# Attention with experts on one Trainium2 core: the values' products start one iteration later

## The chip, the core and the metric

The kernel runs on one core of a Trainium2 chip. The metric is device time in microseconds (us) for one execution; lower is better. The engines are named as in the profile: PE is TensorE (matrix products, with PEld for its weight loads), DVE is VectorE, ACT is ScalarE, POOL is GpSimd and SP is SyncE, which issues most of the DMAs here.

## The reference

The program is an attention layer, a mixture of experts that sends each token to one of eight experts, and a dense layer. The change lies in the attention, for 4 batches, 8 heads, 576 tokens and a head width of 64, all in float32:

```
scores = scale * q @ k.T                      # per batch and head
thresh = max(scores, axis=-1) - tau
scores = where(scores >= thresh, scores, -1e9)
scores = scores - max(scores)
attn   = exp(scores)
attn   = attn / (sum(attn) + 1e-9)
out    = attn @ v
```

The experts and the dense layer then work on the 2304 rows of 512 that come out. They use the rows of all batches, so most of them can't begin before attention is nearly done.

## The kernel before, in words

**Pairs, units, iterations.** Two heads make a pair, so there are 16 pairs (`NPAIR`), four per batch. The 576 tokens of the queries of a pair are cut into 9 units (`UPP`): units 0 to 7 are 128 queries of one head, unit 8 is the last 64 queries of both heads. `run` (L440) walks over 144 units, two per iteration, in 73 iterations. Nine iterations are two pairs, one period. `k = it % 9` is the place in the period.

**What an iteration emits, in this order.** The order is written out by hand, and each engine works off its own instructions in that order.
- At the start of a pair: the loads of a later pair's keys and queries (`load`, tile F, L123) and values (`load_v`, tile V, four buffers, L127), and a note that the operands of a later pair are to be split on GpSimd (`split`, L142) and placed by four DMAs (`place`, L162 to L165, tiles qT, kA and kB).
- `qk` (L229): the scores of this iteration's two units, on TensorE (L244), into four PSUM banks that two units use by turns. A unit's scores wait until the mask of the unit two before has read the banks.
- `trans` (L316): the transposes of the two units of the iteration before (L330) and, for k = 0, 2, 5 and 7, those of the tail tokens (`trans_tails`, L338).
- `max` (VectorE, L272) and `exp` (ScalarE, L278) of both units; then ScalarE copies the transposes out of PSUM to the tiles AT (L332, L334) and ATt (L357), each with two buffers; then `mask` on VectorE (L302).
- `values(n)` (L391): it takes up to n items from the queue `avq` and emits them.
- Row items (`row_items`, L398): TensorE turns the finished columns xT back into rows (L414), ScalarE copies them (L419), GpSimd scales them and SP writes them to DRAM.
- One piece of splitting on GpSimd, and some items of the side queue (router set-up and, later, the router's small operations on VectorE): one per iteration, up to eight in the last part.
- At the end of the iteration, the items of a half are put at the end of `avq`: when the transposes that it needs have been emitted, at unit 5 for the first half and unit 8 for the second.

**The items of a half.** A half is 288 of a pair's 576 query columns. It has five items (`av_items`, L359): four product items, `main(0)` to `main(3)`, and one closing item, `tail`. A product item is two matrix products, one per head, which appear as four instructions with 128 x 64 weights (L374); all add up in one PSUM tile `av`. The closing item is a product with the tail tokens (L380, two instructions with 128 x 128 weights), and then ScalarE's copy of `av` to xT (L381). The PSUM pool of `av` has one buffer (`P("ps_av", 1, space=PSUM)`, L1064), so `main(0)` of the next half has to wait for that copy. The closing item of an odd pair's second half also puts five row items into `rowq`.

**How many items per iteration.** The quotas are tables. From iteration `IT_LAST` = 54 on, `AVL` and `ROWL` replace `AV` and `ROW`:

```
AV = (2, 2, 3, 3, 2, 2, 3, 2, 1)
ROW = (0, 1, 0, 1, 1, 0, 1, 0, 1)
AVL = (2, 2, 3, 5, 0, 2, 3, 2, 1, 2, 2, 3, 5, 0, 2, 3, 3, 2, 5)
ROWL = (1, 1, 1, 0, 1, 1, 1, 1, 1, 0, 0, 0, 0, 1, 1, 1, 1, 1, 1)
```

A period has 20 items, and `AV` adds up to 20, so the queue repeats itself. The first items are put into it at the end of iteration 3. In the first five iterations some transposes of the identity, written into a tile `av`, keep TensorE at work (`FILL`).

What is left in the queues after `run` is taken by `tail` (L510) while the expert part begins.

Of the kernel before, what the change touches and what calls it, by code (L numbers as in the profile page):

```python
# [24 lines left out]
UPP = 9  # L25
PJ = 9
NPC = 2
AV = (2, 2, 3, 3, 2, 2, 3, 2, 1)
TURNS = ((0, 1), (2, 3))
TAILS = {2: -1, 5: -2, 7: -2, 0: -1}  # L30
IT_LAST = (NPAIR - HP) * UPP // 2
AVL = (2, 2, 3, 5, 0, 2, 3, 2, 1, 2, 2, 3, 5, 0, 2, 3, 3, 2, 5)
# [17 lines left out]
class Attention:  # L50
# [389 lines left out]
    def run(self):  # L440
        nc = self.nc
        NU = NPAIR * UPP
        self.load_first()
        self.load(1)
        rest = self.first()
        self.load_v(0)
        self.load_v(1)
        self.load(2)
        self.poolq = []
        self.avq, self.rowq, self.side = avq, rowq, side = [], [], []  # L450
        side += [None] * NS0 + [self.gate_setup, *self.router.setup_items(self.setup), *self.extra]
        it = done = 0
        while done < NU:
            last = it >= IT_LAST
            us = [u for u in (2 * it, 2 * it + 1) if u < NU]
            ts = [u for u in (2 * it - 2, 2 * it - 1) if 0 <= u < NU]
            starts = [u // UPP for u in us if u % UPP == 0]
            for p in starts:
                if p + 3 < NPAIR:
                    self.load(p + 3)  # L460
                if p + 2 < NPAIR:
                    self.load_v(p + 2)
                for n in range(1 if p == 0 else p + 2, min(p + 3, NPAIR)):
                    self.operands(n)
                    self.poolq += [lambda n=n, i=i: self.split(n, i, NPC) for i in range(NPC)]
            k = it % 9
            for u in us:
                self.qk(u)
            copies = [self.trans(u) for u in ts]
            if it > 1 and k in TAILS:  # L470
                copies.append(self.trans_tails(2 * it + TAILS[k]))
            for i in range(2):
                if i < len(us):
                    self.max(us[i])
                    self.exp(us[i])
                if last:
                    self.sides(SD[i], False)
            for c in copies:
                c()
            while rest:  # L480
                rest.pop(0)()
            if self.norm:
                self.norm.pop(0)()
            for i, u in enumerate(us):
                self.mask(u)
                if last:
                    self.sides(SD[i + 2], False)
            if it < len(FILL) and FILL[it]:
                warm = self.ps_av.tile([128, 512], F32, name="av")
                for _ in range(FILL[it]):  # L490
                    nc.tensor.transpose(warm[:, 0:128], self.ident, self.ident)
            n = AVL[it - IT_LAST] if last else AV[k]
            self.values(n)
            m = ROWL[it - IT_LAST] if last else ROW[k]
            while m and rowq:
                rowq.pop(0)()
                m -= 1
            n = 1 if it else 2
            while n and self.poolq:
                self.poolq.pop(0)()  # L500
                n -= 1
            self.sides(SD[4] if last else SN)
            for u in ts:
                done = u + 1
                p, w = divmod(u, UPP)
                if w in (5, 8):
                    avq += self.av_items(p, w // 8)
            it += 1
# [1074 lines left out]
```

## Time and profile before

| what | value |
|---|---|
| time, median of 3 runs | 964.17 us (961.75 to 965.95) |
| the profiled execution's own time | 964.58 us |
| its span, first to last instruction | 962.8 us |
| mean granted TensorE clock | 0.987 of full speed |
| TensorE busy | 910.0 us, 95% of the span |
| VectorE busy | 510.8 us, 53% |
| ScalarE busy | 446.9 us, 46% |
| GpSimd busy | 223.3 us, 23% |

The profile is that of one execution. Its time is 1.8 us longer than its span, since launch and end lie around the instructions. A share of busy time is an average over the whole span, and attention (to about 348 us) and the expert and dense part behind it have different limits. Matrix products are pipelined and their ends are modelled, so a busy TensorE need not be at its peak. An idle time is put down to what ended it by the semaphores that the instruction waited for; "issue" means that the profile shows nothing that it waited for.

### The profile page before, as it was taken

The numbers are of one execution on the slowest core, as the hardware profiler recorded it, in microseconds if no ns is written. First come the engines' busy times: TensorE is split into PE (matmuls) and PEld (weight loads), VectorE is DVE, ScalarE is ACT, GpSimd is POOL, SyncE is SP. The second block draws the span as 40 slices with busy tenths as digits, with TensorE's granted clock in tenths as the row PEclk, the third lists the DMA queues.
The fourth block names the chain that finished last, engine by engine and source line by source line (L and its number), as shares of the span: only waits on it lengthen the run. The fifth ranks groups of instructions, "written<-read, shape, count | busy, mean of one in ns | idle before, by whom it ended". The sixth has DMA issues, their size and how long they took to land.

```text
span 962.8 us, 13873 instructions
## 1 busy us (share of the span) xinstructions
PE 910.0 (95%) x5031; PEld 744.9 (77%) x5031; DVE 510.8 (53%) x1129; ACT 446.9 (46%) x788; POOL 223.3 (23%) x299
## 2 busy tenths in 40 slices
PE   8899899998898989999999999999999999999995
PEld 7677677776676668877888988888888888888894
DVE  6677677776778748457868658851111111111110
ACT  6566666666666543345555544542222222222221
POOL 4737544566441340101151000001001000100100
PEclk9999999999999989999999999999999999999998
DMA  7655565544440262546574625421001000100100
GB/s 213 161 138 138 161 160 143 149 111 121 118 116 12 67 222 91 183 137 229 181 228 154 240 67 175 127 70 44 22 23 45 1 16 6 44 1 1 44 1 24
DMA packets 64522, 100.70 MB, mean 105 GB/s; under 512 B 10596, under 2 KB 35970, under 8 KB 64450
## 3 DMA queue, kind: packets, MB, share of 16 engines
q1 hardware_dynamic: 61138, 89.84, 32.0%
q0 software_dynamic: 3312, 9.94, 3.2%
q8 instruction: 41, 0.67, 0.3%
q14 instruction: 31, 0.25, 0.1%
HBM read 63.97 MB, written 17.11 MB: 84 GB/s over the span
## 4 chain that ended last, share of the span: by engine, by line
PE 73%; issue 8%; DVE 6%; ACT 6%; DMA 3%; POOL 1%; SPq 1%; POOLq 0%; ACTq 0%
PE tr L993 27%; PE sc L1018 18%; PE sc L1037 8%; PE sc L244 7%; PE av L374 6%; PE tr L330 3%; ACT e L278 3%; DVE e L272 2%; PE tr L414 2%; ACT AT L332 1%; DVE E L302 1%; DVE ET L302 1%; PE av L380 1%; DMA xg<-x_dram,igaA 1%; DVE bl L1263 1%
## 5 line engine op out<-in xcount | busy, mean ns | idle before, releaser
L1230 DVE TENSOR_TENSOR hl<-sg,hh 128x512 fp32r<-128x512 f32 (+1 forms) x80 | 51.0, 638 | 259.8 <-ACT hh L1228 259.8
L278 ACT ACTIVATE e<-e,thr 128x576 f32<-128x576 f32 x144 | 109.9, 776 | 93.3 <-DVE e L272 90.0
L272 DVE TENSOR_SCALAR_CACHE_REDUCE e<-sc,taue 128x576 f32<-128x576 f32 x144 | 113.9, 816 | 66.6 <-PE sc L244 65.4
L1227 ACT ACTIVATE sg<-tr 128x512 f32<-128x512 f32 (+1 forms) x80 | 44.3, 554 | 224.9 <-PE tr L993 224.9
L1018 PE MATMUL sc<-wo_h,hh 128*128 128x512 f32 x288 | 112.2, 390 | 0.0
L1018 PE MATMUL sc<-wo_l,hh 128*128 128x512 f32 x288 | 112.2, 390 | 0.0
L1018 PE MATMUL sc<-wo_h,hl 128*128 128x512 f32 x288 | 112.0, 389 | 0.0
L244 PE MATMUL sc<-kA,qT 128*128 128x288 f32 x320 | 99.5, 331 | 7.2 <-DVE E L302 3.8
L302 DVE SCALAR_TENSOR_TENSOR E<-sc,thr,e 128x576 f32<-128x576 f32 x128 | 101.1, 813 | 5.1 <-ACT e L278 3.8
L374 PE MATMUL av<-AT,V 128*64 128x288 f32 x512 | 76.5, 422 | 22.1 <-ACT xT L381 22.0
L244 PE MATMUL sc<-kB,qT 128*128 128x288 f32 x320 | 89.3, 299 | 2.1 <-DMA kB<-kB 1.2
L244 PEld LDWEIGHTS sc<-kA,qT 128*128 128x128 f32 x320 | 61.0, 191 | 27.9 <-DVE E L302 14.8
L993 PE MATMUL tr<-xl,wi_h 128*128 128x512 f32 (+1 forms) x320 | 78.7, 368 | 0.0
L993 PE MATMUL tr<-xh,wi_l 128*128 128x512 f32 (+1 forms) x320 | 78.7, 368 | 0.0
L993 PE MATMUL tr<-xh,wi_h 128*128 128x512 f32 (+1 forms) x320 | 78.6, 368 | 0.0
L374 PEld LDWEIGHTS av<-AT,V 128*64 128x64 f32 x512 | 31.4, 137 | 49.6 <-ACT xT L381 27.9
L330 PE MATMUL tr<-ident,E 128*128 128x128 f32 x512 | 69.4, 277 | 0.0
L332 ACT COPY AT<-tr 128x512 f32<-128x512 f32 x128 | 68.2, 577 | 0.1
L993 PEld LDWEIGHTS tr<-xh,wi_h 128*128 128x128 f32 x320 | 57.6, 188 | 11.1
L993 PEld LDWEIGHTS tr<-xl,wi_h 128*128 128x128 f32 x320 | 56.9, 189 | 10.0
L993 PEld LDWEIGHTS tr<-xh,wi_l 128*128 128x128 f32 x320 | 56.9, 189 | 10.0
L244 PEld LDWEIGHTS sc<-kB,qT 128*128 128x128 f32 x320 | 61.4, 192 | 2.9 <-DVE kB L223 1.3
(220 smaller groups left out, 1592.4 us busy)
## 6 DMA issues: line engine op xcount, KB each, us to landing
ra<-in_moe_w_dram SPq DMA_DIRECT2D x20, 512.0 KB, 3.6
rb<-in_moe_w_dram SPq DMA_DIRECT2D x20, 512.0 KB, 3.8
F<-in_kq_dram SPq DMA_DIRECT2D x15, 640.0 KB, 4.8
cv_raw<-in_moe_w_in_dram SPq DMA_DIRECT2D x16, 512.0 KB, 4.5
cv_raw<-in_moe_w_out_dram SPq DMA_DIRECT2D x16, 512.0 KB, 4.2
V<-in_vp_dram SPq DMA_DIRECT2D x16, 320.0 KB, 5.0
kA<-kA SPq DMA_DIRECT2D x15, 320.0 KB, 3.3
kB<-kB SPq DMA_DIRECT2D x15, 320.0 KB, 3.6
```

The lines of the kernel that those rows point to most:

```text
L244: m = nc.tensor.matmul(self.banks[:, bank, 0:288], l, d[kk][:, c0 + k0:c0 + k0 + 288], start=(i == 0), stop=(i == len(ops) - 1),).ins
L272: self.read(u, nc.vector.tensor_scalar(e, d["sc", w], self.taue[:, 0:1], 3.0e38, op0=ALU.add, op1=ALU.min, accum_out=thr))
L278: self.nc.scalar.activation(d["e", w], d["e", w], ACTF.Exp, bias=d["thr", w][:, 0:1], scale=-1.0)
L302: self.read(u, nc.vector.scalar_tensor_tensor(out=E.rearrange("p (a c) -> p a c", a=2), in0=d["sc", w], scalar=d["thr", w][:, 0:1], in1=d[ ...
L330: nc.tensor.transpose(tp[:, kc * 128:(kc + 1) * 128], E[:, k0 + kc * 128:k0 + (kc + 1) * 128], self.ident)
L332: return lambda: nc.scalar.copy(AT[:, h, :, c * 128:(c + 1) * 128], tp.rearrange("p (k c) -> p k c", k=4))
L374: nc.tensor.matmul(d["av"][h * 64:(h + 1) * 64, 0:288], d["V"][:, h, kc, :], d["AT"][:, h, kc, cols], start=(kc == 0), stop=False, skip_gr ...
L993: nc.tensor.matmul(hps[:, 0:T], w[:, kd, :], blk[x][:, kd, 0:T], start=(i == 0), stop=(i == 11))
L1018: nc.tensor.matmul(y, h[:, cs], w, start=(f == 0 and i == 0), stop=(f == blk["nf"] - 1 and i == 2))
L1037: nc.tensor.matmul(blk["y"][d], w[:, ds], h[:, 0:T], start=(f == 0 and i == 0), stop=(f == last and i == 2))
L1227: nc.scalar.activation(sg, hps, ACTF.Gelu_apprx_sigmoid)
L1230: return [upper, lambda: nc.vector.tensor_sub(hl, sg, hh.bitcast(F32))]
```

## The change

The call of `values` gets a condition. With `UPP` = 9, `UPP // 2` is 4, so iterations 0 to 4 take nothing from the queue. Before iteration 4 the queue is empty in any case; at iteration 4 the kernel before took two items.

```
--- before.py
+++ after.py
@@ -489,8 +489,8 @@
                 warm = self.ps_av.tile([128, 512], F32, name="av")
                 for _ in range(FILL[it]):
                     nc.tensor.transpose(warm[:, 0:128], self.ident, self.ident)
-            n = AVL[it - IT_LAST] if last else AV[k]
-            self.values(n)
+            if it > UPP // 2:
+                self.values(AVL[it - IT_LAST] if last else AV[k])
             m = ROWL[it - IT_LAST] if last else ROW[k]
             while m and rowq:
                 rowq.pop(0)()
```

The tables are the same, and so is every instruction; what moves is the place of the values' items, and with the closing items that of the row items, in the order of the iterations.

## Rows read from the trace of the kernel before

**Rows 1.** The page's first part: busy time, share and instructions of each engine.
```profile
PE 910.0 (95%) x5031; PEld 744.9 (77%) x5031; DVE 510.8 (53%) x1129; ACT 446.9 (46%) x788; POOL 223.3 (23%) x299
```

**Rows 2.** Waits of TensorE, 28 to 261 us: total us, times, longest.
```profile
PE av L374 <- ACT xT L381: 21.5, 12, 1.9
```

**Rows 3.** Stretches: start:end, length, busy us of engines, granted clock, DMA.
```profile
28.28:261.00 232.72, 208.96 (x1472) 161.76 (x1473) 172.88 (x471) 153.33 (x285) 126.87 (x170) 0.99 0.54 139
348.00:963.00 615.00, 601.16 (x2868) 502.81 (x2867) 259.04 (x437) 225.49 (x380) 53.94 (x65) 0.99 0.27 89
```

**Rows 4.** Timeline, one iteration of k = 2: start, duration, instruction, idle time before.
```profile
97.06 0.65 PE L380 MATMUL av<-ATt,V 128*128 128x288 f32 x2
...
97.78 1.05 ACT L332 COPY AT<-tr 128x512 f32<-128x512 f32 x2
...
98.98 0.42 ACT L381 COPY xT<-av 128x288 f32<-128x288 f32 x1
...
99.46 1.19 PE L374 MATMUL av<-AT,V 128*64 128x288 f32 x8 [1.75 <-ACT xT L381]
```

**Rows 5.** Stretches: iterations k = 0, 2, 6, 7 of one period, and its sum.
```profile
127.76:131.86 4.10, 3.92 (x30) 2.88 (x28) 3.78 (x10) 3.76 (x9) 2.34 (x3) 1.00 0.19 60
...
135.60:141.56 5.96, 4.20 (x29) 2.96 (x28) 3.94 (x11) 3.82 (x9) 4.86 (x5) 1.00 0.34 116
...
153.73:159.93 6.20, 4.48 (x33) 3.27 (x31) 4.06 (x12) 3.82 (x8) 5.81 (x5) 1.00 0.02 3
159.93:163.38 3.45, 3.45 (x29) 2.64 (x28) 2.46 (x7) 2.10 (x4) 1.41 (x3) 1.00 0.80 171
...
sum 39.36, PE 35.69 PEld 27.82 DVE 30.01 ACT 26.41 POOL 20.77; mean PE 3.97 PEld 3.09 DVE 3.33 ACT 2.93 POOL 2.31
```

**Rows 6.** Stretches: iterations 60 (k = 6), 65 (k = 2) and 69 (k = 6).
```profile
274.34:278.55 4.21, 4.21 (x33) 3.30 (x32) 3.13 (x8) 3.03 (x7) 4.03 (x5) 1.00 0.08 19
...
294.98:299.38 4.40, 4.12 (x29) 3.02 (x29) 4.37 (x16) 2.86 (x6) 1.01 (x6) 1.00 0.01 4
...
313.90:318.12 4.22, 4.22 (x33) 3.31 (x32) 4.07 (x17) 2.98 (x6) 0.81 (x2) 1.00 0.14 35
```

**Rows 7.** Timeline of iteration 60 and the start of iteration 61.
```profile
276.45 1.19 PE L374 MATMUL av<-AT,V 128*64 128x288 f32 x8
...
277.56 0.30 PEld L380 LDWEIGHTS av<-ATt,V 128*128 128x128 f32 x2 [0.44 <-issue]
277.57 0.75 PE L380 MATMUL av<-ATt,V 128*128 128x288 f32 x2
...
278.16 0.65 PE L414 MATMUL tr<-G,xT 128*128 128x144 f32 x4
278.44 0.41 ACT L381 COPY xT<-av 128x288 f32<-128x288 f32 x1
...
280.29 0.78 ACT L278 ACTIVATE e<-e,thr 128x576 f32<-128x576 f32 x1 [0.99 <-DVE e L272]
...
280.88 1.19 PE L374 MATMUL av<-AT,V 128*64 128x288 f32 x8
```

**Rows 8.** Line L374 from 266 to 330 us: what its idle time ended with.
```profile
  issue: 1.8, 11
```

**Rows 9.** Stretch: iterations 58 to 66 together.
```profile
265.85:304.09 38.24, 35.76 (x259) 28.00 (x257) 30.58 (x85) 26.89 (x50) 13.40 (x22) 1.00 0.31 72
```

**Rows 10.** Stretches by granted clock, and iteration 7 (k = 7).
```profile
39.20:42.60 3.40, 3.40 (x17) 3.29 (x16) 2.47 (x7) 1.64 (x3) 0.82 (x1) 0.50 0.67 147
...
117.70:121.10 3.40, 3.40 (x16) 2.30 (x13) 0.00 (x0) 0.40 (x1) 1.81 (x3) 0.50 0.50 110
...
261.00:264.40 3.40, 3.40 (x18) 3.06 (x18) 2.49 (x7) 1.55 (x3) 1.51 (x1) 0.51 0.59 127
...
38.79:43.86 5.07, 5.07 (x28) 4.19 (x26) 3.24 (x8) 2.78 (x5) 1.23 (x1) 0.66 0.62 134
```

**Rows 11.** Timeline of SP: the last DMA that places pair 6's operands.
```profile
103.68 0.59 SPq L165 DMA_DIRECT2D kB<-kB  x1
```

More of the change, by code (lines that the diff above doesn't have):

```diff
@@ L491, in run @@
                     nc.tensor.transpose(warm[:, 0:128], self.ident, self.ident)
-            n = AVL[it - IT_LAST] if last else AV[k]
-            self.values(n)
+            if it > UPP // 2:
+                self.values(AVL[it - IT_LAST] if last else AV[k])
             m = ROWL[it - IT_LAST] if last else ROW[k]
```

## The prediction, made before the change was run

> **What bounds the kernel now.** I read the page first: TensorE is busy for 910.0 us of a span of 962.8 [rows 1]. A share of 95% looks as if nothing were left, so I asked next who TensorE waited for in the steady part of attention, 28 to 261 us, where the change lies. One wait heads that list: 21.5 us, 12 times, the first product of a half waiting for ScalarE's copy of the half before (L374 behind L381) [rows 2]. The same stretch as a window has 232.72 us with 208.96 us of TensorE in it [rows 3], so this wait is 21.5 of 23.8 us idle.
>
> The timeline of one such iteration shows how it comes about [rows 4]. The closing product starts at 97.06 and takes 0.65 us, so it is over at 97.7. Its copy to xT stands in ScalarE's queue behind the copies of this iteration's transposes, which start at 97.78, and begins only at 98.98. There is one av bank, so the next half's first product, which follows in the same run, starts at 99.46, after 1.75 us idle. A closing product at the *front* of a run meets ScalarE when it still has the iteration's copies to do.
>
> Last I cut one period of nine iterations (39.36 us) into its iterations [rows 5]. I call them by k, the iteration's number modulo 9. Two are long: k = 2 with 5.96 us and k = 6 with 6.20; the other seven have 27.2 us together, 3.9 each. The long ones are those whose run is "closing, first, second".
>
> **The change part by part.** The queue of the values' items starts one iteration later and stays two items behind. With m for a product item and T for a closing one, the runs of a period were k=0 mm, 1 mm, 2 Tmm, 3 mmT, 4 mm, 5 mm, 6 Tmm, 7 mm, 8 T. They become mT, mm, mmT, mmm, mT, mm, mmT, mm, m. The 20 items are all there, T is always last, and no m follows a T in its own run. At iteration 57 the quota of five takes three items before and five after; from its end on the order is the same in both kernels. So from iteration 58 the trace of before holds iterations in just the new order: my price list.
>
> *k = 6, six iterations.* 6.20 us now [rows 5]. The same items with T last took 4.21 and 4.22 us [rows 6]. Saved 1.98 each, 6 x 1.98 = 11.9.
>
> *k = 2, six iterations.* 5.96 us now, with 4.20 us of TensorE [rows 5]; without the wait 4.20 would be left. The iteration of this k in the new order took 4.40, with 0.28 of TensorE idle [rows 6], while VectorE had small operations of the router to do as well. I take 4.30, between the two: 6 x 1.66 = 10.0 (9.4 to 10.6).
>
> *k = 0, 3, 4 and 8* exchange an m for a T or back. Two m take 1.12 us, from 276.45 to 277.57, so one takes 0.56; a T takes 0.59, from 277.57 to 278.16 [rows 7]. Each exchange is 0.03 us, plus in two and minus in two: nothing. If k = 0 lost its 0.18 us of idle TensorE too [rows 5], that would be 6 x 0.18 = 1.1 more.
>
> As a check: a period becomes 39.36 - 1.98 - 1.66 = 35.7 us. The nine iterations from 265.85 to 304.09, with 20 items in the new order, hold 35.76 us of TensorE in 38.24 [rows 9]. The 2.5 us between are idle, in iterations that run up to eight of the router's items; the steady ones run one.
>
> *The clock.* Three stretches of 3.4 us ran at a granted 0.50 or 0.51, the 1.2 GHz level, and each began during or right behind one of the twelve waits, at 39.20, 117.70 and 261.00 [rows 10]. The first made an iteration of k = 7 last 5.07 us [rows 10] where the same k takes 3.45 at full clock [rows 5]: 1.6 each, 4.8 for three. With no idle of 1.8 us left in front of them I take all three as gone; the other end is 0.
>
> *The two ends.* Iteration 4 loses two m, 1.12 us of TensorE, but its next scores also wait for VectorE's masks; the gain is 0 to 1.1, I take 0.6. Iteration 57 gets two m more, +1.1. One row item moves out of iteration 12 and one into 55: nothing. Together +0.5.
>
> *What I cost at nothing, and what covers it.* (a) The copy to xT now ends each run, ahead of the next iteration's exponentials in ScalarE's queue. In the new order it starts at 278.44 and takes 0.41 us, and the next exponential starts at 280.29, after ScalarE was idle for 0.99 [rows 7]. With that cover gone it would be 0.41 per half, 24 halves, 10 us. (b) The first product of the next run meets a copy long done: at 280.88 no copy is named before it [rows 7], and over the whole late stretch the products waited for "issue" alone, 1.8 us [rows 8]. (c) SP: a pair's V load goes into the buffer of the pair four before the pair loaded, whose last closing product now comes in the load's own iteration, not the one before. SP waits there an iteration longer, about 4 us; behind it stand operand placements, row writes and later loads. The placement issued at 103.68 [rows 11] is for the pair that starts at 127.76 [rows 5], so 24 us early. (d) The AT and ATt buffers (two each) are refilled in the iteration after a pair's last T, behind it on TensorE, which works in order. (e) The row items, and the router's behind them, come an iteration or two later until iteration 57, then at the old places. (f) The expert part, 615 us from 348 on [rows 3], starts from what attention delivers and moves up with it; I find nothing in it tied to absolute time.
>
> One price the notes would add. In the trace a T behind an m has its weight load idle for 0.44 us, but its matmul starts at 277.57, just when eight at 0.14 are through, so TensorE loses nothing [rows 7]. The Trainium skill (TensorE: Matmul & The Clock Gate, Part 3, The mechanism) says that a weight load overlaps matmuls in flight only when the row groups differ, which speaks against full-array products behind half-array ones. One more such switch comes per period (at k = 8): by the rule 6 x 0.44 = 2.6 us and a time near 941; by the row, 0.
>
> **Sum.** -11.9 - 10.0 - 4.8 + 0.5 = -26.2 against this execution's own 964.58 us (its span is 962.8): 938.4. The execution lies 0.4 above the median of the runs shown, 964.17, so 938.
>
> **The rivals.**
> 1. *The clock falls all the same*, there or elsewhere: 964.6 - 21.9 + 0.5 = 943. For: nine of the twelve waits had no fall behind them, so such a wait alone does not decide it. Against: all three falls touch a wait.
> 2. *VectorE takes over.* Periods then look like the 38.24 us of [rows 9], 1.1 saved each: 964.6 - 6.7 - 4.8 + 0.5 = 954. For: VectorE is busy 30.0 us of 39.36 [rows 5] and would be so of 35.7. Against: the steady part has one side item per iteration, and its plain iteration reaches 3.45 [rows 5].
> 3. *The wait only moves* to the next iteration's first product, so that the change does not do what it says: 960 to 965. For: there is still one av bank. Against: the late stretch [rows 8]. The Trainium skill (Perfetto Trace Analysis, Optimizing Tensor Performance, Matmuls) asks that independent groups rotate through banks, so that one's evacuation overlaps the next one's matmuls; by that rule an unrotated bank keeps its wait. The late stretch does not agree: scores and transposes fill the time.
> 4. *Slower: SP's queue.* The V load that waits an iteration longer holds back the operand placements behind it. Place: SP at a pair's start. Price, if a pair's scores had to wait for that iteration: 13 pairs x 4 us = 52, so 938 + 52 = 990. It decides only once the hold exceeds the 24 us by which a placement is early.
>
> **How the numbers follow.** Forecast 0.66, rival 1 0.16, rival 2 0.09, rival 3 0.06, rival 4 0.03. Predicted: 938. The range goes down by 1.1 for k = 0, 0.6 for the end of k = 2 and about 2 for half-clock stretches elsewhere that also touch an idle TensorE: 934. Upward it takes in rival 1 (943) and 4 us of rival 2's waits: 947. About 0.2 is outside. No change means within 0.5%, 4.8 us, about what a measurement can tell: rival 3. Faster 0.91, same 0.06, slower 0.03.
>
> **What would show it.** In the profile after: TensorE's wait for the xT copy gone from the steady part (if it stands before the next iteration's products, rival 3); k = 2 and k = 6 at 4.2 to 4.4 us (longer, and idle behind VectorE's masks: rival 2); no stretch at 0.50 between the first values and iteration 57 (else rival 1); no wait of the scores for an operand's DMA after iteration 4 (else rival 4). The expert part must keep its length; if it changes by more than 2 us, point (f) is wrong.

## The result, and the profile after

The changed kernel takes 936.49 us (934.96 to 938.53, median of 4 runs) against 963.83 us in runs beside it; the ratio is 0.9725 with a 95% interval of 0.9697 to 0.9753. The prediction was 938. The profiled execution took 936.12 us with a span of 934.4, so 28.5 us less than the one of before.

The page's first part of the changed kernel, which answers to [rows 1]: the same instructions, TensorE 6 us less busy.

```profile
PE 904.0 (97%) x5031; PEld 740.6 (79%) x5031; DVE 512.2 (55%) x1129; ACT 446.8 (48%) x788; POOL 223.1 (24%) x299
```

TensorE's waits in the changed kernel from 28.79 to 238.64 us (iterations 5 to 57). This is the whole list; the row of [rows 2] is no longer in it.

```profile
PE sc L244 <- DVE E L302: 0.7, 3, 0.3
PE sc L244 <- DVE ET L302: 0.5, 2, 0.3
PE sc L244 <- issue: 0.2, 1, 0.2
```

The same as stretches (length, then busy us of each engine). The steady part has 1.0 us without TensorE where [rows 3] had 23.8. The second row is the expert and dense part, from its first product to the end.

```profile
28.79:233.92 205.13, 204.10 (x1463) 159.00 (x1463) 173.70 (x469) 152.02 (x283) 123.42 (x165) 1.00 0.62 157
319.45:934.40 614.95, 600.95 (x2867) 502.91 (x2867) 257.63 (x435) 224.94 (x378) 52.33 (x65) 0.99 0.28 89
```

The timeline of the changed kernel's iteration 20 (k = 2), the one of [rows 4].

```profile
89.12 1.19 PE L374 MATMUL av<-AT,V 128*64 128x288 f32 x8
...
89.95 1.06 ACT L332 COPY AT<-tr 128x512 f32<-128x512 f32 x2
...
90.24 0.75 PE L380 MATMUL av<-ATt,V 128*128 128x288 f32 x2
...
90.61 0.51 PE L244 MATMUL sc<-kA,qT 128*128 128x288 f32 x1
...
90.89 0.38 ACT L357 COPY ATt<-tr 128x256 f32<-128x256 f32 x1
...
90.96 0.29 PE L244 MATMUL sc<-kB,qT 128*128 128x288 f32 x1
...
91.16 0.42 ACT L381 COPY xT<-av 128x288 f32<-128x288 f32 x1
```

The closing product (L380) comes after the two product items, and the next scores follow it at 90.61. ScalarE's copy to xT still stands behind its other copies; it starts 0.92 us after the closing product (1.92 in [rows 4]), and TensorE has scores and transposes to do meanwhile.

One period of the changed kernel (iterations 27 to 35, k = 0 to 8), to be read beside [rows 5].

```profile
114.56:118.32 3.76, 3.76 (x29) 2.94 (x28) 3.59 (x10) 3.07 (x7) 2.53 (x3) 1.00 0.94 253
118.32:122.18 3.86, 3.86 (x30) 3.00 (x29) 3.41 (x10) 3.08 (x7) 2.45 (x3) 1.00 0.73 154
122.18:126.01 3.83, 3.83 (x32) 2.97 (x30) 3.46 (x10) 2.87 (x6) 2.80 (x4) 1.00 0.76 275
126.01:130.34 4.33, 4.33 (x35) 3.31 (x33) 3.58 (x11) 3.43 (x7) 2.17 (x2) 1.00 0.51 109
130.34:134.62 4.28, 4.28 (x31) 3.57 (x31) 2.74 (x7) 2.39 (x6) 0.95 (x3) 1.00 0.90 195
134.62:138.29 3.67, 3.67 (x31) 2.87 (x29) 3.06 (x9) 3.01 (x7) 2.35 (x3) 1.00 0.91 255
138.29:142.52 4.23, 4.23 (x32) 3.32 (x31) 4.06 (x10) 3.13 (x7) 3.98 (x4) 1.00 0.23 82
142.52:145.97 3.45, 3.45 (x29) 2.65 (x27) 2.69 (x10) 2.53 (x6) 3.30 (x4) 1.00 0.24 51
145.97:149.97 4.00, 4.00 (x31) 3.23 (x29) 3.34 (x10) 2.80 (x6) 0.27 (x2) 1.00 0.86 189
sum 35.41, PE 35.41 PEld 27.87 DVE 29.93 ACT 26.32 POOL 20.80; mean PE 3.93 PEld 3.10 DVE 3.33 ACT 2.92 POOL 2.31
```

The period went from 39.36 to 35.41 us, and TensorE is busy in all of it. Over the whole execution, the end of iteration 57 comes 27.2 us earlier (265.85 before, 238.64 now); from there to the first product of the experts 1.9 us are gained (82.76 and 80.81 us), and the part behind takes 0.8 us more (614.19 and 614.95): 28.4 us of span.

### The profile page after: what moved, and what is told of

It reads as the page before. It is cut to its first block, busy times and chain, and to the rows that moved or that the text cites. A ratio compares the mean times of both kernels' runs of the same rounds, so it can differ in the third digit from the quotient of the medians.

```text
span 934.4 us, 13874 instructions
## 1 busy us (share of the span) xinstructions
PE 904.0 (97%) x5031; PEld 740.6 (79%) x5031; DVE 512.2 (55%) x1129; ACT 446.8 (48%) x788; POOL 223.1 (24%) x299
## 4 chain that ended last, share of the span: by engine, by line
PE 81%; issue 7%; DVE 4%; DMA 3%; ACT 2%; POOL 2%; SPq 1%; POOLq 0%; ACTq 0%
PE tr L993 28%; PE sc L1018 19%; PE sc L1037 9%; PE sc L244 8%; PE av L374 6%; PE tr L330 5%; PE av L380 2%; PE tr L414 2%; DVE e L272 1%; ACT e L278 1%; DMA cv_raw<-in_moe_w_in_dram 1%; SPq L179 1%; PE tr L352 1%; DVE E L302 1%; DMA xg<-y_first 1%
## 5 line engine op out<-in xcount | busy, mean ns | idle before, releaser
L374 PE MATMUL av<-AT,V 128*64 128x288 f32 x512 | 76.9, 419 | 0.5 <-ACT xT L381 0.5
L1018 PEld LDWEIGHTS sc<-wo_h,hl 128*128 128x128 f32 x288 | 54.0, 188 | 11.4
```

What stands on the lines that cost most here:

```text
L374: nc.tensor.matmul(d["av"][h * 64:(h + 1) * 64, 0:288], d["V"][:, h, kc, :], d["AT"][:, h, kc, cols], start=(kc == 0), stop=False, skip_gr ...
L1018: nc.tensor.matmul(y, h[:, cs], w, start=(f == 0 and i == 0), stop=(f == blk["nf"] - 1 and i == 2))
```

## The experiments

My theory: a closing item at the front of a run queues its copy on ScalarE behind the iteration's other copies, and with one av bank the next product has to wait; at the end of a run other matmuls cover it. Rivals: the one bank itself is the wait, wherever the copy stands; or the products gain because they come later. In the edits, "..." stands for lines and table entries that are not shown.

**The changed kernel again**, as the measure for the next three.

> The changed kernel once more, as the measure for the other three. All theories: 936 us, a ratio of 0.972 to the kernel before, and in the trace no wait of the products for the xT copy before the last pair. One open point rides on it: the first trace of the changed kernel had no half-clock stretch at all before the end, although only those three were expected to go that touched the twelve waits. If the falls come from idle TensorE alone, none is seen in the steady part again; if they also come by chance, one or two are, and the time is 2 to 3 us longer.

Measured: 936.52 us (935.2 to 939.54), ratio 0.9729 (0.9706 to 0.9752). Up to the experts this trace had one stretch at half clock, 3.4 us at 313.8, behind the steady part; between the first values and iteration 57 there was none. Falls in the steady part went with its waits; those at the end of attention come and go between executions.

**Closing items last, same start.** Only the tables change:

```
-AV = (2, 2, 3, 3, 2, 2, 3, 2, 1)
+AV = (2, 3, 2, 3, 2, 2, 1, 2, 3)
-AVL = (2, 2, 3, 5, 0, 2, ...)
+AVL = (2, 3, 2, 5, 0, 2, ...)
```

> The queue starts at iteration 4 as before, but the quotas are changed so that each closing item ends its run (runs mm, mmT, mm, mmT, mm, mm, T, mm, mmT for k = 0 to 8). Theory (a closing item at the front of a run queues its copy behind ScalarE's other copies, at the end it does not): the twelve waits are gone, 21.9 us with 4.8 us of clock; the load is spread less evenly (k = 8 near 5.0 us, k = 6 held at 3.45 by VectorE), which gives back about 0.8 us per period, 5 us: 938 to 943. Rival (what helps is that the products come an iteration later and find their inputs long ready): the start is the old one, so no gain: 960 to 966.

Measured: 938.83 us (936.35 to 939.69), ratio 0.9742 (0.9721 to 0.9763). The whole list of TensorE's waits in this kernel from 28 to 240 us:

```profile
PE sc L244 <- DVE E L302: 1.6, 4, 0.8
PE tr L414 <- ACT AT L332: 0.3, 1, 0.3
```

No product waits for a copy, though the queue starts as early as before. So the gain does not need the later start; it comes with the order within a run. A period takes 35.96 us, with 4.76 at k = 8 and 3.45 at k = 6, where 5.0 and 3.45 were expected.

**Half of it.** The quotas of k = 6 and k = 8 are exchanged, and k = 2 keeps "closing, first, second":

```
-AV = (2, 2, 3, 3, 2, 2, 3, 2, 1)
+AV = (2, 2, 3, 3, 2, 2, 1, 2, 3)
```

> The kernel before with the quotas of k = 6 and k = 8 exchanged (1 and 3), so the closing item of an even pair's first half is alone in its run and that of its second half ends one, while k = 2 still has closing, first, second. Theory: one of the two waits per period is gone, six of twelve: 6 x 1.98 = 11.9 less, about 2 us back for the longer k = 8, one or two falls of the clock fewer: 950 to 954, half of the gain. Rival (it needs the whole shift): 960 or more.

Measured: 949.08 us (947.26 to 950.34), ratio 0.9863 (0.9835 to 0.9892), a shade better than expected: half of the change's gain. Of the waits the six at k = 2 are left; the row from 28 to 251 us:

```profile
PE av L374 <- ACT xT L381: 11.3, 6, 2.0
```

**One item instead of two.** The same kind of edit, but the queue stays one item behind, so that a product follows a closing item in four runs of a period:

```
             n = AVL[it - IT_LAST] if last else AV[k]
+            if it <= UPP // 2:
+                n = 1
             self.values(n)
```

> The kernel before with one item taken at iteration 4 instead of two, so the queue stays one item behind, not two. Runs: k = 0 Tm, 1 mm, 2 mTm, 3 mm, 4 ... so that a product follows a closing item in its own run at k = 0, 2, 4 and 6. Theory: four waits per period instead of two; at k = 2 and k = 6 the closing item is 0.5 us later in the run and the wait as much shorter (1.2 to 1.4), at k = 0 and k = 4 there are new ones of 1.7 to 1.9: about 6 us per period instead of 3.6, 6 periods, +14 us, and as many falls of the clock or more: 974 to 982, slower than before. Rival (later products help by themselves): half of the gain of the change, 950.

Measured: 976.86 us (975.44 to 981.0), ratio 1.0158 (1.0121 to 1.0195): slower, as the theory says and against "later helps". The row from 28 to 285 us has 23 waits:

```profile
PE av L374 <- ACT xT L381: 32.0, 23, 1.9
```

They are 1.6 us at k = 0, 1.1 at k = 2 and 6 and 1.9 at k = 4. Where the closing item stands one item later in its run, the wait is shorter.

**The copy first.** Where a closing item leads a run, it is emitted before the copies of the transposes:

```
+            n = AVL[it - IT_LAST] if last else AV[k]
+            if n > 1 and avq and avq[0].__name__ == "tail":
+                n -= 1
+                self.values(1)
             for c in copies:
                 c()
...
-            n = AVL[it - IT_LAST] if last else AV[k]
             self.values(n)
```

> The kernel before, with one thing moved: where a closing item leads a run, it is emitted before the iteration's copies of the transposes, so that its copy to xT stands in front of them in ScalarE's queue. TensorE's order and the runs stay the same (closing, first, second). Theory (the wait is the queue on ScalarE): the copy starts when the second exponential ends, at 97.9 instead of 98.98 in the iteration of the trace, and the wait shrinks from 1.75 to about 0.7 us: 12 x 1.1 = 13 us less and one to three falls of the clock fewer, 946 to 951. Rival (with one bank the round trip TensorE, ScalarE, TensorE is the wait, wherever the copy stands): no change, 960 to 965.

Measured: 944.8 us (943.92 to 945.8), ratio 0.9821 (0.9795 to 0.9846), about 1 us better than the expected range. Its iteration 20, where [rows 4] had the xT copy 1.2 us behind the first AT copy:

```profile
90.42 1.52 ACT L278 ACTIVATE e<-e,thr 128x576 f32<-128x576 f32 x2 [1.13 <-DVE e L272]
...
91.13 0.65 PE L380 MATMUL av<-ATt,V 128*128 128x288 f32 x2
91.84 0.38 ACT L381 COPY xT<-av 128x288 f32<-128x288 f32 x1
92.12 1.07 ACT L332 COPY AT<-tr 128x512 f32<-128x512 f32 x2
92.28 0.68 PEld L374 LDWEIGHTS av<-AT,V 128*64 128x64 f32 x8 [0.95 <-ACT xT L381]
92.28 1.19 PE L374 MATMUL av<-AT,V 128*64 128x288 f32 x8 [0.49 <-ACT xT L381]
```

The copy now starts when the exponentials and the closing product end, and the wait falls from 1.75 to 0.49 us here, and over the twelve from 21.5 to 8.2. So some 13 us of the wait were ScalarE's copies of the transposes. The other 8 are not all the way over ScalarE: at k = 6 the copy still stands behind the exponentials. In iteration 15 the closing product is over at 70.92, and the copy starts at 71.41:

```profile
70.27 0.65 PE L380 MATMUL av<-ATt,V 128*128 128x288 f32 x2
...
71.41 0.38 ACT L381 COPY xT<-av 128x288 f32<-128x288 f32 x1
...
71.84 0.95 PE L374 MATMUL av<-AT,V 128*64 128x288 f32 x6 [0.92 <-ACT xT L381]
```

With 0.49 us at k = 2 taken as the way over ScalarE, twelve times, about 6 us are the one bank and about 2 more the queue (an estimate from these rows). Both are parts of the wait; of the versions tried, only those with other matmuls behind the closing product remove both.

**The idle time filled.** Ten transposes of the identity into unused columns of the av bank, in front of the copy; they add nothing to the output. The flag `more`, set in `values`, says that the run goes on behind this item, and `filling` that `run` is not over:

```
+            if self.more and self.filling:
+                for _ in range(10):
+                    nc.tensor.transpose(d["av"][:, 320:448], self.ident, self.ident)
             nc.scalar.copy(xT[:, cols], d["av"][:, 0:288])
...
```

> The kernel before with ten transposes of the identity (0.11 us each) into unused columns of the av bank, between a closing product that does not end its run and its copy. They add nothing to the output. They fill 1.1 of the 1.75 to 1.9 us for which TensorE is idle, and the copy could not start earlier in any case. It sets the clock's share by itself. Theory (the half-clock stretches follow from the idle time): the waits shrink to 0.6 to 0.8 us each but iterations keep 5.96 and 6.20 us, no stretch at 0.50 before the last pair, time 4 to 5 us under the kernel before: 959. Rival (the falls are not due to these waits): 964, with three or so stretches at 0.50 left.

Measured: 960.75 us (958.67 to 961.88, 12 runs) against 963.42 (17 runs), ratio 0.9966 (0.9949 to 0.9982). The waits shrank as planned, and the iterations kept their length (5.98 at k = 2, 6.21 at k = 6). The row of this kernel from 28 to 262 us, and its stretch to 300 us with the granted clock in third place from the end (1.00), above the one of the kernel before in the profile of the prediction (0.98):

```profile
PE av L374 <- ACT xT L384: 8.5, 12, 0.8
```

```profile
28.00:300.00 272.00, 258.72 (x1878) 204.50 (x1875) 205.98 (x563) 182.30 (x338) 142.04 (x192) 1.00 0.52 132
```

```profile
28.00:300.00 272.00, 245.71 (x1725) 190.75 (x1723) 203.76 (x556) 180.32 (x335) 142.06 (x192) 0.98 0.52 132
```

No stretch at half clock is left before 335 us, and the mean granted clock has a median of 0.993 over its runs, against 0.988 for the kernel before beside it. So the falls do follow from the idle time. The other traces fit: before 300 us there is no fall with twelve waits of 0.5 to 0.9 us (the copy first), one with six of 1.7 to 2.0 (half of it) and three with 23 of 0.9 to 1.9 (one item). In the filled kernel the falls are worth 3.3 us (1.7 to 4.9), a little under the 4 to 5 expected, which the interval takes in.

**Fewer runs of products**, made from the changed kernel:

```
-AV = (2, 2, 3, 3, 2, 2, 3, 2, 1)
+AV = (2, 2, 3, 4, 1, 2, 3, 3, 0)
```

> The changed kernel with the items gathered into fewer runs of products: k = 4 has the closing item alone and k = 8 none, their products go to k = 3 (four) and k = 7 (three). Two switches between full-array and half-array weights fewer per period. Theory that a switch costs TensorE 0.25 us (k = 8 got 0.24 us longer when its closing item was exchanged for a product): 12 x 0.25 = 3 us less, 933, if VectorE lets k = 4 and k = 8 get shorter. Theory of the prediction's row (a switch costs TensorE nothing): 936, unchanged. If VectorE sets k = 8 at 3.5 to 3.6 us, about half is seen: 934.5.

Measured: 940.55 us (939.04 to 940.64), ratio 0.976 (0.974 to 0.978), slower than the changed kernel beside it (0.9729), which none of the three expectations gave. One period of it, iterations k = 0, 3, 4, 5, 7, 8 and the sum:

```profile
114.97:118.96 3.99, 3.81 (x27) 2.92 (x27) 3.77 (x10) 3.35 (x8) 2.53 (x3) 1.00 0.95 262
...
126.65:131.45 4.80, 4.80 (x38) 3.58 (x36) 3.58 (x11) 3.43 (x7) 2.16 (x2) 1.00 0.60 130
131.45:135.43 3.98, 3.71 (x27) 3.39 (x26) 2.44 (x7) 2.08 (x4) 0.95 (x3) 1.00 0.90 200
135.43:139.33 3.90, 3.90 (x28) 2.93 (x28) 3.58 (x9) 3.52 (x8) 2.28 (x3) 1.00 0.90 276
...
143.59:147.52 3.93, 3.93 (x33) 2.93 (x31) 2.96 (x8) 2.89 (x7) 3.59 (x5) 1.00 0.32 66
147.52:151.09 3.57, 3.23 (x27) 3.04 (x25) 2.68 (x9) 2.08 (x5) 0.00 (x0) 1.00 0.86 188
sum 36.12, PE 35.33 PEld 28.11 DVE 29.98 ACT 26.41 POOL 20.76; mean PE 3.93 PEld 3.12 DVE 3.33 ACT 2.93 POOL 2.31
```

Against the changed kernel, k = 3 and k = 7 grow by 0.47 and 0.48 us, the price of one product item; k = 4 and k = 8 give back 0.30 and 0.43, and then TensorE is idle in them and at k = 0 (0.8 us per period); k = 0 and k = 5, which follow the emptied iterations, are 0.23 longer. TensorE's waits for VectorE's masks and for "issue" rise from 1.4 to 5.9 us. The balance of the runs matters more than their number; what a switch would cost if nothing else were late was not settled by this.

No version tried beats the changed kernel. A second av bank was not tried; as written, the kernel has four PSUM banks for the scores, three tiles for the transposes and one for av.

## Why the prediction was right

Forecast 938.4 for the profiled execution, measured 936.1. Step by step:

- *k = 6.* Predicted 1.98 each; measured 6.20 to 4.23, 1.97. The price list from the same trace held: iterations 58 to 70 are the same in both traces to 0.02 us each.
- *k = 2.* Predicted 1.66 each; measured 1.87 to 2.16, 12.2 us in place of 10.0. The 4.20 us of busy TensorE that I took as a floor was too long. In [rows 4] the closing product counts 0.65 us, since idle time follows; in the changed kernel the next matmul starts 0.37 us behind it (90.24 to 90.61). That is 0.28 of the 0.37 us between 4.20 and the 3.82 or 3.83 that three of the six iterations take. A busy share next to a wait holds the tail of a pipeline that nothing follows. A part of it only moves on: the first score matmul behind the closing product is followed by the second after 0.35 us (90.61 to 90.96), and by 0.24 where a product item stands in front, in the kernel before:

```profile
100.58 0.40 PE L244 MATMUL sc<-kA,qT 128*128 128x288 f32 x1
...
100.82 0.29 PE L244 MATMUL sc<-kB,qT 128*128 128x288 f32 x1
```
- *The exchanges at k = 0, 3, 4 and 8.* Predicted nothing. Measured: k = 0 gained up to 0.34 each, 1.6 us in all, beyond the 1.1 that I had kept for the range; k = 8 lost 1.4, and k = 1, which I had not named, 0.8. k = 3 lost 0.1 in each of four iterations, and iteration 12, from which a row item went, gained 0.4 where I had put nothing. Most of the loss at k = 1 and k = 3 is the 0.11 us just shown, since both now follow a closing product. The net loss is about 0.6 us, but k = 8 is a size that I had wrong: 3.75 became 4.00. Its products and weight loads in iteration 17, first before, then after:

```profile
84.75 1.03 PE L330 MATMUL tr<-ident,E 128*128 128x128 f32 x8
...
85.52 0.30 PEld L380 LDWEIGHTS av<-ATt,V 128*128 128x128 f32 x2
85.62 0.65 PE L380 MATMUL av<-ATt,V 128*128 128x288 f32 x2
...
85.87 0.68 PEld L414 LDWEIGHTS tr<-G,xT 128*128 128x128 f32 x4
...
86.11 0.65 PE L414 MATMUL tr<-G,xT 128*128 128x144 f32 x4
```

```profile
76.94 1.04 PE L330 MATMUL tr<-ident,E 128*128 128x128 f32 x8
...
77.90 0.20 PEld L374 LDWEIGHTS av<-AT,V 128*64 128x64 f32 x4 [0.17 <-issue]
77.90 0.71 PE L374 MATMUL av<-AT,V 128*64 128x288 f32 x4
...
78.53 0.54 PEld L414 LDWEIGHTS tr<-G,xT 128*128 128x128 f32 x4 [0.44 <-issue]
78.54 0.76 PE L414 MATMUL tr<-G,xT 128*128 128x144 f32 x4
```

  The transposes to the item take 0.87 us before and 0.96 after, the item 0.49 and 0.64. A product item behind another costs 0.48 (0.64 for one alone, 1.12 for two in [rows 7]); the first one of a run costs 0.16 more, and 0.09 go by before it. I had divided a run of two by two and so spread that cost over both. The Trainium skill's rule (TensorE: Matmul & The Clock Gate, Part 3, The mechanism), which I weighed with 0.44 per switch against a measured 0, has the sign of this loss: the trace gives 0.24. The trace does not agree with the rule as I put it, since between full-array products the loads start before their matmuls (85.52 before 85.62, 85.87 before 86.11); around the lone product item they start with them (77.90; 78.53 and 78.54). That the weight loads cause the 0.24 is not shown.
- *The clock.* Predicted 4.8 in the profiled execution; iteration 7 gives back 1.5, iterations 24 and 25 together 1.6 beyond the wait, and no stretch is left in the steady part. The third stretch, in iteration 57, gave back about 1.4 (an estimate: 0.47 less, with two more items of 0.48). Two of the three falls began 1.5 us after their wait had ended (at 37.66 and 259.54), so that "right behind" said more than the rows; what ties them to the waits is the filled kernel, which puts them at 3.3 (1.7 to 4.9) over many runs.
- *The two ends.* Predicted +0.5: iteration 4 gained 0.76 of which iteration 5 lost 0.47; iteration 57 takes 4.72 with its two extra items.
- *What I cost at nothing.* (a) and (b): the list of waits above. (c): no wait for an operand's DMA in the steady part; SP, which I had waiting about 4 us at each pair, waited for a values' buffer twice, 4.1 us in all (L127, to 300 us). (f): 614.95 us against 614.19, under the 2 us that I had allowed.
- *Not foreseen:* 1.9 us between iteration 57 and the experts. Before, TensorE ran at half clock for 6.8 us from 339.5 on; in this trace not at all. The experiments' traces have 3.4 to 6.8 us there, so it varies with the execution.

That the sum came within 2.3 us is in part luck: k = 2, k = 0 and the stretch ahead of the experts gained some 5.7 us that were not in it, and k = 8, k = 1, k = 3 and the expert part lost 3.4. The two large terms, the twelve waits, were right in their mechanism.

Rival 1 fails on the changed kernel's two traces, which have no fall before 313 us, rival 2 on the period that TensorE fills, rivals 3 and 4 on the waits. The Trainium skill's advice on rotating banks (Perfetto Trace Analysis, Optimizing Tensor Performance, Matmuls) names a real cost here, about 6 of the 8 us of wait in the kernel with the copy first; the changed kernel's trace shows that independent matmuls behind the closing product hide it without a second bank.

## What to carry to other kernels

Where one accumulator bank is reused and other matmuls follow, end a burst with the product that closes it, so that they run while it is copied out; and look at what its copy queues behind on the copying engine. When a trace already has some iterations in the new order, price the change from them rather than from busy times next to a wait. Moving one item in such a queue can turn the sign: two items later gained 2.7%, one item later lost 1.6%.

## What the runs showed of the hardware

In the kernel before, twelve idle times of 1.72 to 1.90 us on TensorE, in 233 us, brought three stretches of 3.4 us at the 1.2 GHz level in the profiled execution. With ten transposes of 0.11 us each in every such gap, which leave 0.64 to 0.81 us idle, the granted clock stayed at the 2.4 GHz level in that stretch. One product item (four matmuls with 64-column weights) alone between full-width matmuls cost 0.24 us more than a closing product (two full-width matmuls) in its place.
